# Transposing x by VectorE from a second load in 128-byte pieces: batches 2 and 3 of a fused attention and two-layer MLP kernel

## The chip, the cores and the metric

One core of a Trainium2 chip runs the kernel. The metric is the device time in microseconds (us) of one execution; of several runs the median is given. TensorE, VectorE, ScalarE, GpSimd (POOL) and SyncE (SP) each run their own queue of instructions in order, and wait for each other by semaphores. In the profile PE is TensorE's matmuls, PEld its weight loads, DVE is VectorE, ACT is ScalarE. DMAs are issued from the queues of SP and POOL.

## The reference

Attention between x and a small state in both directions, then two MLPs over all tokens, all in float32.

```python
# x: 4 x 8 x 512 x 64 (batch, head, token, channel), state: 4 x 8 x 32 x 64
scores  = softmax(x @ state.T / 8)        # per batch and head, 512 x 32
xread   = scores @ state                  # 512 x 64
scores2 = softmax(state @ x.T / 8)        # 32 x 512
sread   = scores2 @ x                     # 32 x 64
a = concat([xread, sread], axis=2)        # to 2176 tokens x 512
h = a @ moe_w_in;   a = (h - tanh(h)) @ moe_w_out          # 512 -> 2048 -> 512
h = a @ moe2_w_in;  out = (h * tanh(softplus(h))) @ moe2_w_out
```

## The kernel before

**The first half.** Work runs in steps. A step is one entry of the list `seq`: a batch b and one of 16 slices t of the hidden dimension of the first MLP. Batch 0 has steps 0 to 15, batch 1 steps 16 to 31, batch 2 steps 32 to 47; then come four steps for the state tokens and 16 for batch 3. In each step TensorE runs six matmuls into `h` (`up_x`, which reads the attention weights `ath`, `atl`) and twelve into four accumulators `acc0` to `acc3` (`down_x`, three steps behind). ScalarE computes tanh (`t`) and the rounded large part `gh`; VectorE computes h - tanh(h) (also `t`, or `wide` where the tile is half of a wide one) and the rest `gl`. At a batch's last step the four accumulators are copied to `y` (ScalarE acc0 and acc2, VectorE acc1 and acc3, `evac`). `h` alternates between two banks of PSUM; side work has two banks.

**Side work** is hung on the steps: `at(step, function)`. The attention of batches 2 and 3 is prepared while batch b - 1 runs, by the steps in `when[b]`, counted from that batch's first step (`start`). Of that preparation:

- `load_x(b)` loads x into four tiles `x`, one for each pair of heads k, by POOL.
- `at_xt(b, k)` transposes a tile: `xt_t` runs four 128x128 matmuls against an identity into a side bank `xtp`, `xt_c` copies the bank to `xt` (ScalarE, for batches 2 and 3).
- `sc_m(b)` computes the scores by sixteen 64x32 matmuls, alternating between two side banks (e = 0 and 1; `sct`), `sc_c` copies them to `scs`.
- `at_exp`, `at_norm`, `at_exp_t`, `at_read_t` and `at_sread` make both softmaxes and `sread` (`e2p`, `srd`); `sw` multiplies the state into the first weights (`swp`, split into `swh` and `swl` for the two banks). Only `at_sread` needs the x tile as it was loaded.

Weights of the second MLP are converted meanwhile: SP loads them to three stage buffers `st` (`load_next`), ScalarE reads a buffer twice (`w`, `r`), VectorE joins the two, and POOL stores the split parts (`wh`, `wl`) to DRAM (`wi`, `wo`). A load into a stage buffer waits until ScalarE has read what stood there. SBUF is kept in slots (`get`, `put`): a tile that takes a slot waits for those who last used it. DMAs of SP use eight semaphores in turn, so one waits until the eighth before it has landed.

**The second half** is the second MLP in 16 groups (`group`, `downs`), with weights loaded back from DRAM (`ws`, `wo`).

The order on each engine is that of a scheduler which follows the order of the code by priority; inside `sc_m` the matmuls after the first have a raised priority.

Of the kernel before, what the change touches and what calls it, by code (L numbers as in the profile page):

```python
# [10 lines left out]
F32 = mybir.dt.float32  # L11
# [65 lines left out]
def attention_moe_kernel(  # L77
# [10 lines left out]
    nc = tc.nc  # L88
# [5 lines left out]
    KD = DM // 128  # L94
# [3 lines left out]
    def order(after, before, cls=mybir.DependencyClass.NoSync):  # L98
        tc.add_manual_dep(
            after, before.name,  # L100
            mybir.DependencyInfo(cls, mybir.DependencyReason.DATA),
            reason="order of work",
        )

    TE, AC, V = (Pinned(e, order) for e in (nc.tensor, nc.scalar, nc.vector))
# [10 lines left out]
    free, halves = deque(range(NSLOT)), deque()  # L116
    wide = [slots.tile([128, 1024], F32, tag=f"v{i}", name="wide") for i in range(WIDE)]

    def get(name, dtype=F32, newest=False):
        if halves and dtype == F32:  # L120
            return halves.popleft()
        i = free.pop() if newest else free.popleft()
        return Unit(slots.tile([128, 512], dtype, tag=f"k{i}", name=name), i)

    def put(*units):
        for u in units:
            if u.slot is None:
                halves.append(u)
            else:
                free.append(u.slot)  # L130
# [4 lines left out]
    def side_bank(name):  # L135
        ps_n[0] += 1
        return psum.tile([128, 512], F32, tag=banks[ps_n[0] % len(banks)], name=name)

    ident = misc.tile([128, 128], F32, name="ident")
    SB = get("sbt")  # L140
    XS = get("xst")
    xst = XS.t.rearrange("p (k n) -> p k n", k=KD)

    SX = get("sx")

    def head(b, k, i, half=None):
        c = (b * KD + k) * NS
        p = i if half is None else half
        return (SB if p == i else SX).t[p * 64:(p + 1) * 64, c:c + NS]
# [259 lines left out]
    XT, SC, ET = {}, {}, {}  # L409

    def load_x(b, ks=range(KD)):
        for k in ks:
            u = get("x", newest=b > 1)
            (nc.gpsimd if b > 1 else nc.sync).dma_start(
                out=u.t.rearrange("p (h c) -> p h c", h=2),
                in_=x[b, 2 * k:2 * k + 2].rearrange("h (p r) d -> p h (r d)", r=4),
            )
            X[b, k] = u
# [5 lines left out]
    P = {}  # L424

    def v3(u):
        return u.rearrange("p (g n) -> p g n", n=NS)

    def xt_t(b, k):
        P["x", b, k] = ps = side_bank("xtp")  # L430
        for r in range(4):
            TE.transpose(
                out=ps[:, r * 128:(r + 1) * 128],
                in_=X[b, k].t[:, r * 128:(r + 1) * 128],
                identity=ident,
            )

    def xt_c(b, k):
        XT[b, k] = get("xt")
        evac(XT[b, k].t, P.pop(("x", b, k)), 0 if b else k)  # L440

    def at_xt(b, k):
        xt_t(b, k)
        xt_c(b, k)

    def sc_m(b):


        P["c", b] = [side_bank("sct") for _ in range(2)]
        before = None  # L450
        for i in range(2):
            for k in range(KD):
                for e in range(2):
                    with tc.high_priority() if before else nullcontext():
                        mm = TE.matmul(
                            out=P["c", b][e][k * NS:(k + 1) * NS, i * 256:(i + 1) * 256],
                            lhsT=head(b, k, i, e),
                            rhs=XT[b, k].t[e * 64:(e + 1) * 64, i * 256:(i + 1) * 256],
                            start=True,
                            stop=True,  # L460
                        ).ins
                    if before:
                        order(mm, before)
                    before = mm
        put(*(XT.pop((b, k)) for k in range(KD)))

    def sc_c(b, i):
        SC[b, i] = get("scs")
        for e in range(2):
            evac(  # L470
                SC[b, i].t.rearrange("p (q e n) -> p q e n", q=2, e=2)[:, :, e, :],
                P["c", b][e][:, i * 256:(i + 1) * 256].rearrange("p (q n) -> p q n", q=2),
                e if b else 1 - i,
            )

    def at_scores(b):
        sc_m(b)
        for j in range(2):
            sc_c(b, j)
# [34 lines left out]
    def at_exp(b, j):  # L514
        sc_t(b, j)
        sc_max(b, j)
        sc_sub(b, j)
        sc_exp(b, j)
# [19 lines left out]
    def at_norm(b, j):  # L538
        nm_sum(b, j)
        nm_rec(b, j)  # L540
        nm_mul(b, j)

    def at_exp_t(b, j):
        e = SC.pop((b, j))
        mt = small.tile([128, 2], F32, tag="mt", name="mt")
        V.tensor_reduce(out=mt[:, 0:1], in_=e.t, axis=AX.X, op=ALU.max)
        V.tensor_scalar(
            out=mt[:, 0:1], in0=mt[:, 0:1], scalar1=-scale, scalar2=None, op0=ALU.mult
        )
        AC.activation(  # L550
            out=e.t, in_=e.t, func=ACTF.Exp, scale=scale, bias=mt[:, 0:1], accum_out=mt[:, 1:2]
        )
        V.tensor_scalar(
            out=mt[:, 1:2], in0=mt[:, 1:2], scalar1=1e-9, scalar2=None, op0=ALU.add
        )
        V.reciprocal(out=mt[:, 1:2], in_=mt[:, 1:2])
        V.tensor_scalar(
            out=e.t, in0=e.t, scalar1=mt[:, 1:2], scalar2=None, op0=ALU.mult
        )
        ET[b, j] = e  # L560

    def at_read_t(b, j):
        ps = side_bank("e2p")
        e = ET.pop((b, j))
        for r in range(4):
            TE.transpose(
                out=ps[:, r * 128:(r + 1) * 128],
                in_=e.t[:, r * 128:(r + 1) * 128],
                identity=ident,
            )  # L570
        u = get("e2")
        AC.activation(out=u.t, in_=ps, func=ACTF.Copy)
        put(e)
        ET[b, j] = u
# [19 lines left out]
    def at_sturn(b):  # L594
        ps = side_bank("srt")
        u = P.pop(("r", b))
        TE.transpose(out=ps[:, :128], in_=u.t[:, :128], identity=ident)
        put(u)
        V.tensor_copy(
            out=xst[:, :, b * NS:(b + 1) * NS],  # L600
            in_=ps[:, :128].rearrange("p (k n) -> p k n", k=KD),
        )

    def at_steps(b):
        st = [lambda k=k: at_xt(b, k) for k in range(KD - 1)]
        return st + [
            lambda: at_xt(b, KD - 1),
            lambda: at_scores(b),
            lambda: (at_exp(b, 0), at_exp_t(b, 0)),
            lambda: at_norm(b, 0),  # L610
            lambda: (at_exp(b, 1), at_exp_t(b, 1), at_read_t(b, 0)),
            lambda: at_norm(b, 1),
            lambda: at_read_t(b, 1),
            lambda: at_sread(b),
            lambda: at_sturn(b),
        ]

    def at_a_hi(b, j):
        a = A.pop((b, j))
        if b >= TURN:  # L620
            u = get("at")
            V.transpose(out=u.t, in_=a.t)
            src = u.t
        else:
            u, src = None, side_bank("atp")
            for r in range(4):
                TE.transpose(
                    out=src[:, r * 128:(r + 1) * 128],
                    in_=a.t[:, r * 128:(r + 1) * 128],
                    identity=ident,  # L630
                )
        put(a)
        h = get("ath", F32R)
        last[0] = AC.activation(out=h.t, in_=src, func=ACTF.Copy).ins
        AT.setdefault(b, []).append((h, src, u))
# [85 lines left out]
    def evac(dst, src, i):  # L721
        if i % 2:
            return V.tensor_copy(out=dst, in_=src)
        return AC.activation(out=dst, in_=src, func=ACTF.Copy)
# [370 lines left out]
    def at(step, fn, back=None):  # L1095

        def held():
            kept = [e.floor for e in engines]
            for e, m in zip(engines, marks[-back]):
                e.floor = m  # L1100
            fn()
            for e, m in zip(engines, kept):
                e.floor = m

        side.setdefault(step, []).append(held if back else fn)

    seq = []
    start = {}
# [16 lines left out]
    for j in range(2):  # L1125
        at(12 + j, lambda j=j: at_exp(1, j))
        at(13 + j, lambda j=j: at_norm(1, j))
        for b in range(2):
            k = start[1] + 4 + 2 * b + 4 * j
            at(k, lambda b=b, j=j: at_exp_t(b, j), 1)  # L1130
            at(k + 3 - b, lambda b=b, j=j: at_read_t(b, j), 1)
            if j:
                at(k + 4 - b, lambda b=b: at_sread(b), 1)
                at(k + 5, lambda b=b: at_sturn(b), 1)
    when = {2: (3, 4, 5, 7, 8, 9, 10, 11, 12, 13, 15, 16), 3: (3, 3, 4, 5, 7, 8, 9, 11, 12, 12, 13, 15)}
    for b in (2, 3):
        at(start[b - 1] - (b - 2), lambda b=b: load_x(b))
        for i, f in zip(when[b], at_steps(b), strict=True):
            at(start[b - 1] + i, f)
    for b in (1, 2, 3):  # L1140
# [57 lines left out]
    st = {}  # L1198
# [145 lines left out]
```

## Time and profile before

| | |
|---|---|
| median of 3 runs (lowest, highest) | 709.61 us (708.37, 709.80) |
| the profiled execution's own time | 709.34 us |
| its span in the trace | 707.6 us |
| TensorE (PE) busy | 697.7 us, 99% of the span |
| VectorE, ScalarE, GpSimd busy | 472.7, 351.2, 70.7 us |
| mean DMA rate | 168 GB/s |

The time is the span and 1.7 us around it. Busy times of PE overlap: matmuls are pipelined, and one of 512 columns that takes 390 ns in the trace starts 227 ns after the one before it.

### The profile page before, as it was taken

To read this page: it belongs to the slowest core of one execution; us is meant where nothing else is said; L and a number is where in the kernel's file an instruction comes from. 1 tells how busy PE (TensorE), PEld (TensorE's weight loads), DVE (VectorE), ACT (ScalarE), POOL (GpSimd) and SP (SyncE) were. 2 spreads that over 40 slices of the span, in tenths; PEclk is the share of its full clock that TensorE was granted. 3 is DMA by queue.
4 is the path that set the end of the run, shared out by engine and by line. 5 is a ranking of instruction groups with operands and counts; after the bars stand their busy time and mean duration, and the time that the engine had idled before them with its cause. 6 is when DMAs were issued, how large, how long until landed. Compare 5 with 4: busy or idle time off the path is not lost.

```text
span 707.6 us, 10475 instructions
## 1 busy us (share of the span) xinstructions
PE 697.7 (99%) x3930; PEld 558.1 (79%) x3930; DVE 472.7 (67%) x809; ACT 351.2 (50%) x631; POOL 70.7 (10%) x110
## 2 busy tenths in 40 slices
PE   8899999999999999999999999999999999999998
PEld 6467777788777898778878888888888888888886
DVE  5899955778469757998466875557653456544654
ACT  6999544566575656866555432224333223212320
POOL 0000010006112423401213000000000000000000
PEclk9999999999999999999999999999999999999999
DMA  8985110017454568574949645443966345322003
GB/s 283 357 281 195 60 60 2 31 45 230 158 173 141 208 221 283 200 279 140 367 177 329 209 150 165 150 134 125 317 209 197 112 136 176 120 78 74 1 0 134
DMA packets 52643, 118.66 MB, mean 168 GB/s; under 512 B 7280, under 2 KB 11632, under 8 KB 52592
## 3 DMA queue, kind: packets, MB, share of 16 engines
q1 hardware_dynamic: 44272, 90.72, 38.0%
q0 software_dynamic: 8320, 27.27, 10.7%
q8 instruction: 31, 0.51, 0.3%
q14 instruction: 20, 0.16, 0.1%
HBM read 88.34 MB, written 29.62 MB: 167 GB/s over the span
## 4 chain that ended last, share of the span: by engine, by line
PE 84%; ACT 7%; DVE 5%; issue 1%; DMA 1%; SPq 1%; ACTq 0%; DVEq 0%
PE acc L64 47%; PE h L64 31%; ACT r L64 2%; ACT w L64 2%; PE hs L64 2%; PE swp L64 2%; DVE wide L64 1%; DMA x<-in_x_dram 1%; PE xtp L64 1%; DVE wl L64 1%; ACT gh L64 1%; DVE w L64 1%; ACT wide L64 1%; ACT t L64 1%; PE srd L64 1%
## 5 line engine op out<-in xcount | busy, mean ns | idle before, releaser
L64 PE MATMUL acc<-wo,gh 128*128 128x512 f32 (+1 forms) x548 | 168.0, 388 | 0.0
L64 PE MATMUL h<-yh,ws 128*128 128x512 f32 x448 | 156.7, 391 | 0.1
L64 PEld LDWEIGHTS acc<-wo,gh 128*128 128x128 f32 x548 | 102.1, 188 | 21.0 <-ACT gh L64 0.4
L64 DVE TENSOR_TENSOR wide<-acc,wide 128x512 f32<-128x512 f32 (+1 forms) x92 | 63.0, 684 | 74.5 <-PE acc L64 73.2
L64 PE MATMUL acc<-wo,gl 128*128 128x512 f32 (+1 forms) x274 | 106.3, 388 | 0.0
L64 PE MATMUL acc<-gh,wh 128*128 128x512 f32 x244 | 98.7, 404 | 0.0
L64 PEld LDWEIGHTS h<-yh,ws 128*128 128x128 f32 x448 | 84.1, 188 | 17.7 <-DVE mt L64 0.5
L64 PE MATMUL acc<-gh,wl 128*128 128x512 f32 x244 | 95.6, 392 | 0.0
L64 PE MATMUL acc<-gl,wh 128*128 128x512 f32 x244 | 95.1, 390 | 0.0
L64 PE MATMUL h<-yl,ws 128*128 128x512 f32 x224 | 87.2, 389 | 0.0
L64 DVE TENSOR_TENSOR wide<-h,wide 128x512 f32<-128x512 f32 x94 | 64.7, 688 | 25.1 <-PE h L64 13.2
L64 DVE TENSOR_TENSOR gl<-wide,gh 128x512 fp32r<-128x512 f32 x72 | 49.7, 691 | 47.4 <-ACT gh L64 47.2
L64 ACT ACTIVATE wide<-wide 128x512 f32<-128x512 f32 x47 | 29.7, 632 | 85.4 <-DVE wide L64 85.4
L64 ACT ACTIVATE wide<-h 128x512 f32<-128x512 f32 x41 | 24.4, 596 | 78.6 <-PE h L64 76.3
L64 PEld LDWEIGHTS acc<-wo,gl 128*128 128x128 f32 x274 | 51.4, 188 | 11.0 <-DVE gl L64 0.4
L64 PEld LDWEIGHTS acc<-gh,wh 128*128 128x128 f32 x244 | 45.8, 188 | 18.1 <-issue 4.6
L64 PEld LDWEIGHTS acc<-gh,wl 128*128 128x128 f32 x244 | 45.8, 188 | 11.3 <-issue 1.2
L64 PE MATMUL h<-ath,swh 128*128 128x512 f32 x128 | 51.6, 403 | 2.0 <-DVE t L64 1.0
L64 PEld LDWEIGHTS acc<-gl,wh 128*128 128x128 f32 x244 | 45.9, 188 | 8.6
L64 PE MATMUL h<-ath,swl 128*128 128x512 f32 x128 | 50.5, 395 | 0.1
L64 PE MATMUL h<-atl,swh 128*128 128x512 f32 x128 | 49.9, 390 | 0.0
L64 PEld LDWEIGHTS h<-yl,ws 128*128 128x128 f32 x224 | 42.1, 188 | 8.5
(175 smaller groups left out, 1019.6 us busy)
## 6 DMA issues: line engine op xcount, KB each, us to landing
ws<-wi SPq DMA_DIRECT2D x128, 256.0 KB, 3.8
wo<-wo SPq DMA_DIRECT2D x64, 256.0 KB, 3.8
st<-in_moe_w_in_dram SPq DMA_DIRECT2D x27, 512.0 KB, 5.7
st<-in_moe_w_out_dram SPq DMA_DIRECT2D x22, 512.0 KB, 4.9
wi<-wh POOLq DMA_DIRECT2D x32, 256.0 KB, 3.4
wi<-wl POOLq DMA_DIRECT2D x32, 256.0 KB, 4.6
wide<-in_moe_w_out_dram SPq DMA_DIRECT2D x10, 512.0 KB, 5.2
wo<-wh POOLq DMA_DIRECT2D x16, 256.0 KB, 5.8
```

Source lines behind the costliest of these rows:

```text
L64: i = fn(*args, **kw)
```

## The change

For batches 2 and 3 TensorE no longer transposes x. `load_xq` loads x a second time, in eight DMAs for each tile, all from SP: each fills 32 partitions with 256 pieces of 128 bytes, so that rows and columns of x stand in 32x32 blocks in places from which one VectorE transpose of 32x32 blocks (`xt_q`) makes `xt`, up to the order of the tokens. The copy of the scores (`sc_c`) puts the tokens back into order. The plain load of x, which `at_sread` still needs, comes eight steps later. In `sc_m` the two banks change places (e = 1 first) for these batches. In batch 3 the last three transposes stand one step later, and the first two no longer share one. The tiles `xq` and `at` don't take halves of wide tiles.

```diff
-    def get(name, dtype=F32, newest=False):
-        if halves and dtype == F32:
+    def get(name, dtype=F32, newest=False, whole=False):
+        if halves and dtype == F32 and not whole:
             return halves.popleft()
...
+    def load_xq(b, k):
+        u = get("xq", whole=True)
+        v = u.t.rearrange("p (i g d) -> p i g d", i=2, g=8)
+        for i in range(2):
+            src = x[b, 2 * k + i].rearrange("(l g e) (c d) -> (e c) l g d", g=8, e=2, c=2)
+            for c in range(4):
+                nc.sync.dma_start(out=v[c * 32:(c + 1) * 32, i], in_=src[c])
+        P["q", b, k] = u
+
+    def xt_q(b, k):
+        u = P.pop(("q", b, k))
+        XT[b, k] = get("xt")
+        V.transpose(out=XT[b, k].t, in_=u.t)
+        put(u)
...
-    def at_xt(b, k):
-        xt_t(b, k)
-        xt_c(b, k)
...
-                for e in range(2):
+                for e in (1, 0) if b > 1 else (0, 1):
...
                 e if b else 1 - i,
+            ) if b < 2 else evac(
+                SC[b, i].t.rearrange("p (q e l h) -> p q e l h", q=2, e=2, h=4)[:, :, e],
+                P["c", b][e][:, i * 256:(i + 1) * 256].rearrange("p (h q l) -> p q l h", h=4, q=2),
+                e,
             )
...
-        st = [lambda k=k: at_xt(b, k) for k in range(KD - 1)]
-        return st + [
-            lambda: at_xt(b, KD - 1),
+        return [lambda k=k: xt_q(b, k) for k in range(KD)] + [
             lambda: at_scores(b),
...
-            u = get("at")
+            u = get("at", whole=True)
...
-    when = {2: (3, 4, 5, 7, 8, 9, 10, 11, 12, 13, 15, 16), 3: (3, 3, 4, 5, 7, 8, 9, 11, 12, 12, 13, 15)}
+    when = {2: (3, 4, 5, 7, 8, 9, 10, 11, 12, 13, 15, 16), 3: (3, 4, 5, 6, 7, 8, 9, 11, 12, 12, 13, 15)}
     for b in (2, 3):
-        at(start[b - 1] - (b - 2), lambda b=b: load_x(b))
+        for k in range(KD):
+            at(start[b - 1] + when[b][k] - 3, lambda b=b, k=k: load_xq(b, k))
+        at(start[b - 1] + 8 - (b - 2), lambda b=b: load_x(b))
```

**TensorE at the scores of batch 2** (step 24; `h_1471` and `h_1479` are the same h before and after, `sct_1499`, `sct_1516` the bank that is written first). Before:

```order
L64 MATMUL h_1471<-ath_1140,swl_1409 128x512
L64 MATMUL e2p_1485<-ident_75,scs_373 128x128 x4
L64 MATMUL sct_1499<-wide_72,sbt_76 32x256
L64 MATMUL acc0_1293<-gh_1357,wh_629 128x512
L64 MATMUL acc0_1293<-gl_1358,wh_629 128x512
L64 MATMUL sct_1500<-wide_72,sx_78 32x256
L64 MATMUL sct_1499<-wide_72,sbt_76 32x256
```

and with the change:

```order
L64 MATMUL h_1479<-ath_1140,swl_1422 128x512
L64 MATMUL e2p_1493<-ident_75,scs_373 128x128 x4
L64 MATMUL acc0_1307<-gh_1375,wh_629 128x512
L64 MATMUL acc0_1307<-gl_1376,wh_629 128x512
L64 MATMUL acc0_1307<-gh_1375,wl_630 128x512
L64 MATMUL acc1_1308<-gh_1375,wh_629 128x512
L64 MATMUL sct_1516<-wide_72,sx_78 32x256
L64 MATMUL sct_1515<-wide_72,sbt_76 32x256
```

Before, two acc matmuls stood between the first sct matmul and the other fifteen; now four acc matmuls stand ahead of all sixteen.

**VectorE at the end of batch 1** (steps 34 and 35; `y` is the copied accumulator, `xq_2102` batch 3's tile k = 1). Before:

```order
L64 TENSOR_TENSOR swl_2136<-swp_2122,swh_2135 128x512
L64 TENSOR_TENSOR gl_2118<-wide_72,gh_2117 128x512
L64 TENSOR_TENSOR swl_2132<-swp_2121,swh_2131 128x512
L64 COPY y_2146<-acc1_1294 128x512
L64 COPY y_2156<-acc3_1296 128x512
L64 SCALAR_TENSOR_TENSOR w_2204<-w_2204,r_2205 128x512
```

and with the change:

```order
L64 TENSOR_TENSOR swl_2163<-swp_2149,swh_2162 128x512
L64 TENSOR_TENSOR gl_2145<-wide_72,gh_2144 128x512
L64 TENSOR_TENSOR swl_2159<-swp_2148,swh_2158 128x512
L64 COPY wide_72<-acc1_1308 128x512
L64 STREAM_TRANSPOSE xt_2270<-xq_2102 128x512
L64 COPY y_2191<-acc3_1310 128x512
L64 SCALAR_TENSOR_TENSOR w_2236<-w_2236,r_2237 128x512
```

A transpose, and with it the wait for xq_2102's DMAs, now stands ahead of the copy of acc3.

**SP from batch 1's first steps to batch 2's fourth** (`xq_1178`, `1216`, `1268`, `1343` are k = 0 to 3 of batch 2, `xq_2053`, `2102`, `2166`, `2209` those of batch 3, `st` weight loads). Before, the loads st_950, 993, 1041, 1125 and 1537 followed each other here. With the change:

```order
L193 DMA st_950<-in_moe2_w_in_dram 128x1024
L437 DMA xq_1216<-in_x_dram 32x8x32 x2
L437 DMA xq_1178<-in_x_dram 32x8x32 x8
L437 DMA xq_1216<-in_x_dram 32x8x32 x6
L437 DMA xq_1268<-in_x_dram 32x8x32 x8
L437 DMA xq_1343<-in_x_dram 32x8x32 x8
L193 DMA st_993<-in_moe2_w_in_dram 128x1024
L193 DMA st_1041<-in_moe2_w_out_dram 128x1024
L437 DMA xq_2166<-in_x_dram 32x8x32 x8
L437 DMA xq_2209<-in_x_dram 32x8x32
L437 DMA xq_2053<-in_x_dram 32x8x32
L193 DMA st_1125<-in_moe2_w_out_dram 128x1024
```

The next rows are st_1553, xq_2053 x7, xq_2102 x8, xq_2209 x5, st_1779, one of xq_2209, st_2024, st_2033 and the last of xq_2209. So all of batch 2's pieces stand between two weight loads, and those of batch 3 stand among the loads and behind what these wait for.

## Rows read from the trace of the kernel before

**Rows 1.** The page, part 1: busy time, share and instructions of each engine.

```profile
PE 697.7 (99%) x3930; PEld 558.1 (79%) x3930; DVE 472.7 (67%) x809; ACT 351.2 (50%) x631; POOL 70.7 (10%) x110
```

**Rows 2.** Windows: PE, PEld, DVE, ACT, POOL busy (count), clock, DMA, GB/s.

```profile
103.00:137.00 34.00, 34.00 (x197) 26.13 (x196) 21.02 (x45) 18.54 (x37) 0.00 (x0) 1.00 0.06 17
171.00:209.00 38.00, 38.00 (x225) 28.97 (x224) 22.19 (x39) 21.90 (x41) 8.98 (x14) 1.00 0.50 173
```

**Rows 3.** Timeline of PE (start, duration): first h of steps 16, 17, 19, 20.

```profile
90.62 0.39 PE L64 MATMUL h<-ath,swh 128*128 128x512 f32 x1
94.70 0.39 PE L64 MATMUL h<-ath,swh 128*128 128x512 f32 x1
...
104.12 0.39 PE L64 MATMUL h<-ath,swh 128*128 128x512 f32 x1
108.70 0.39 PE L64 MATMUL h<-ath,swh 128*128 128x512 f32 x1
```

**Rows 4.** Timeline of PE: step 35 and the start of step 36.

```profile
185.21 0.39 PE L64 MATMUL h<-ath,swh 128*128 128x512 f32 x1
...
186.34 0.39 PE L64 MATMUL h<-ath,swl 128*128 128x512 f32 x1
...
187.37 0.47 PE L64 MATMUL acc<-gh,wh 128*128 128x512 f32 x1
...
190.21 0.39 PE L64 MATMUL h<-ath,swh 128*128 128x512 f32 x1
```

**Rows 5.** Timeline of PE: step 24 and the start of step 25.

```profile
128.15 0.39 PE L64 MATMUL h<-ath,swh 128*128 128x512 f32 x1
...
130.04 0.62 PE L64 MATMUL sct<-wide,sbt 64*32 64x256 f32 x2
...
134.71 0.39 PE L64 MATMUL h<-ath,swh 128*128 128x512 f32 x1
```

**Rows 6.** Timeline of PE: first h of steps 39 and 40.

```profile
204.66 0.39 PE L64 MATMUL h<-ath,swh 128*128 128x512 f32 x1
...
209.99 0.39 PE L64 MATMUL h<-ath,swh 128*128 128x512 f32 x1
```

**Rows 7.** Lines by form (busy us, mean ns), and one tile's (ns min/median/max).

```profile
L64 DVE STREAM_TRANSPOSE a<-wide 128x512 f32<-128x512 f32 x2 | 1.4, 707 | 0.8 <-PE h L64 0.8
L64 ACT ACTIVATE xt<-xtp x6: 592/594/606, 115.3 to 196.8; 128x512 f32<-128x512 f32 x6
```

**Rows 8.** Timeline of DVE: t of steps 19 and 20; copies to y.

```profile
106.38 0.69 DVE L64 TENSOR_TENSOR wide<-h,wide 128x512 f32<-128x512 f32 x1 [1.25 <-ACT wide L64]
...
110.95 0.69 DVE L64 TENSOR_TENSOR wide<-h,wide 128x512 f32<-128x512 f32 x1
...
184.94 1.28 DVE L64 COPY y<-acc 128x512 f32<-128x512 f32 x2
```

**Rows 9.** Tile x: SP's issues (ns), landing; DMA from 1.5 to 2.5 us.

```profile
L414 SPq DMA_DIRECT2D x<-in_x_dram x8: 462/562/1516, 1.2 to 8.0; - x8
DMA to landing us min/median/max: 3.0/4.7/7.8
q1 hardware_dynamic: 523, 0.13, 58.2%
```

**Rows 10.** The page, part 3: packets, MB, share of 16 engines.

```profile
q1 hardware_dynamic: 44272, 90.72, 38.0%
```

**Rows 11.** Timeline of PE: last h of step 15, first of step 22.

```profile
87.68 0.39 PE L64 MATMUL h<-ath,swl 128*128 128x512 f32 x1
...
117.81 0.39 PE L64 MATMUL h<-ath,swh 128*128 128x512 f32 x1
```

**Rows 12.** Timeline of SP's queue, 149 to 170 us: three loads merged.

```profile
150.02 19.43 SPq L193 DMA_DIRECT2D st<-in_moe_w_out_dram  x3
```

**Rows 13.** DMA issues, 160 to 186 us: KB each, median us to landing.

```profile
x<-in_x_dram POOLq DMA_DIRECT2D x3, 256.0 KB, 7.7
wide<-in_x_dram POOLq DMA_DIRECT2D x1, 256.0 KB, 6.9
```

## The prediction

> **What bounds the kernel now.** I read the page first, then the windows, then TensorE's timeline. TensorE is busy for 697.7 of 707.6 us [rows 1]. In the two stretches in which batches 2 and 3 are prepared, 103 to 137 and 171 to 209 us, it is busy for every microsecond at the full granted clock (1.00, the 2.4 GHz level), while VectorE is busy for 21.0 of 34 and 22.2 of 38 us [rows 2]. So in these stretches time goes only if TensorE's instructions go, and it is lost only if TensorE is made to wait. Idle VectorE or DMA time saved would be worth nothing.
>
> The period of a step shows what an instruction of TensorE costs, better than its own duration, since matmuls overlap. A plain step (12 matmuls into acc, 6 into h) runs from 90.62 to 94.70, 4.08 us; step 19, with one group of four x transposes, from 104.12 to 108.70, 4.58 us [rows 3]. Step 35 has two groups in a row: 185.21 to 190.21, 5.00 us [rows 4]. So a group costs about 0.48 us, and the second of a pair 0.44.
>
> **What is removed from TensorE.** Eight groups: three alone in batch 2 and one behind an e2p group (which I count as a second of a pair), a pair and two alone in batch 3. That is 5 x 0.48 + 0.44 + 0.92 = 3.76 us. I see no gain beyond that, and little below it: what follows a group in the queue simply moves up.
>
> **The scores.** In batch 2 they are split today: one sct matmul starts at 130.04, two acc matmuls slip in, then the other fifteen run. Step 24 takes 6.56 us, 128.15 to 134.71 [rows 5]. Batch 3 has the scores in one piece and no e2p group: step 39 takes 5.33 us, 204.66 to 209.99 [rows 6]. With 0.48 for the e2p group, an unsplit step 24 would take 5.81, so the split costs 0.75 us. In the changed order four acc matmuls come first and all sixteen sct follow together. That removes the split: bound 0 (the wait for the bank stays) to 0.75; I take 0.75, because four acc matmuls are 0.9 us of cover for the one copy that the first sct waits for.
>
> **What is added beside TensorE.** VectorE gets eight 128x512 transposes at 0.71 us each, 5.7 us; ScalarE loses eight copies of 0.59 us [rows 7]. VectorE has 12.98 and 15.81 us free in the two stretches, so their sum costs nothing; only their places count. What it costs to read the scores in a new element order no row shows: between nothing and, as a bound, one transpose more for each of the eight reads, 0.71 us; they are off TensorE and have several steps of cover, so I take nothing.
>
> One place has no cover. At the end of batch 1 VectorE copies acc1 and then acc3 to y, from 184.94 to 186.22 [rows 8]. Step 35's h ends 0.23 us after its last start at 186.34, at 186.57, and today two transpose groups follow, so that acc starts at 187.37 [rows 4]. Batch 2's first acc is acc3. With the groups gone acc3 is wanted at 186.57, and the order puts a transpose between the two copies: acc3 is then free at about 184.94 + 3 x 0.62 + 0.1 = 186.9. I charge 0.35 us of wait (bounds 0 and 0.7).
>
> **The loads.** Each tile of x comes a second time as eight DMAs of 32 KB, 256 pieces of 128 bytes, all on SP. SP is in order, and a piece waits for the landing of the eighth DMA before it. Call p the time per 32-KB DMA at which this stream runs. Issue bounds it below: SP's issues of x tiles, which also have 256 descriptors, take 0.46 at least, 0.56 in the median; I take 0.56. Data alone gives less: in the stretch in which the state's 256-byte pieces come, 523 packets keep 16 engines 58.2% busy for 1 us, 17.8 ns each, so 256 take 0.28 us [rows 9]. Eight in flight with a landing of 4.7 us (median for x tiles [rows 9]) give 0.59. The far end is a mean packet of the HW queue, 38.0% of 16 x 707.6 us over 44272 packets, 97 ns: 256 of them take 1.55 us [rows 10]. That packet has 2 KB, so I stand near the low end.
>
> In batch 2 all 32 DMAs stand together. The first tile is held until step 15's h ends, 87.68 + 0.23 = 87.9 [rows 11]. The tile with least room is xq_1268, the 24th DMA: 87.9 + 24 x 0.56 + 4.7 = 106.0, and VectorE wants it after t of step 19, at 107.1 [rows 8]. Being late costs nothing at first: t of step 20 ends at 111.6 [rows 8], and its bank is wanted by step 22's h at 117.8 [rows 11], 6.2 us of cover.
>
> In batch 3 fifteen DMAs of k = 0 and 1 are queued behind the load st_1553, which waits for ScalarE to have read a stage buffer. Its counterpart today is issued by 169.45, the end of the group of three [rows 12]. So xq_2102 lands at 169.5 + 15 x 0.56 + 4.7 = 182.6, and VectorE wants it at 184.94 + 0.62 = 185.6, just before the acc3 copy. 3 us of room, and behind them no cover. The last piece of k = 3 stands behind st_2033, which waits for a conversion by ScalarE in step 35; VectorE wants it behind gl of step 36, a step (4.1 us) later, against a landing of 4.7: late by half a microsecond, with a step of cover through the h banks. The plain load of x (POOL), now later, serves only srd, six steps or more on.
>
> Here the Trainium skill speaks against the change: "DMA: Bandwidth & Descriptors", Specifications, wants 512 bytes per piece for line rate, and its Rules for kernel authors say that under 64 KB one pays mostly overhead. The trace agrees as far as it goes: 256 bytes in 17.8 ns are 14 GB/s an engine, 2 KB in 97 ns are 21; no row shows 128-byte pieces. If I took that page's 0.95 us for a 64 KB transfer (its section Bandwidth, Measured) for each of these DMAs, an estimate, the sum would end where it began, near 709.
>
> **Sum**, on the profiled execution's 709.34 us (span 707.6 and 1.74 around it; the median of the runs is 0.27 higher): 709.34 - 3.76 - 0.75 + 0.35 = 705.2; half the offset of the median gives **705.3 us**, 0.6% faster.
>
> **Rivals.**
> *A little late (13%).* In 160 to 186 us x tiles took 6.9 and 7.7 us to land beside the stores [rows 13]. Eight in flight at 6.9 give p = 0.86, and xq_2102 lands at 169.5 + 12.9 + 6.9 = 189.3, 3.7 late, all of it on TensorE: 708.9. At 5.8, between: p = 0.73, 186.2, 0.6 late, 705.8. For it: this stretch has the stores. Against: today's slow landings are whole 256-KB tiles, and these four plain loads have left the stretch.
>
> *Slower (8%).* The small pieces themselves are the limit. With p = 1.55, xq_1268 lands at 129.8, 22.7 late less 6.2 of cover, and xq_2102 at 197.5, 11.9 late: 705.2 + 16.5 + 11.9 = 733.6. It decides from p near 0.95: then xq_1268 is 8.3 late, 2.1 beyond its cover, xq_2102 is 2.9 late, and 5.0 lost is more than the 4.2 won. Against: the 256-byte row is at 0.28.
>
> *The gain does not arrive (9%).* TensorE speeds up but meets ScalarE or VectorE waits that the slower pace hid, above all where ScalarE converts weights in order in front of tanh (st_1779 and st_2024 are used soon after they are issued). Half the gain lost gives 707.3, all 709.4. Against: no such wait stands in either stretch now, and an h bank has over a step of room.
>
> **Chances.** Forecast 70%, between 704.3 and 706.3 on its own. A measurement of this kernel tells about 0.2%, 1.4 us, from no change. Faster takes the forecast, and about half of "late" and of "does not arrive": 0.82. Same: the rest of these two, 0.10. Slower: 0.08. For 8 in 10 I give 704.0 to 708.2: below, the waits at nought and 0.4 of run-to-run spread; above, half of the two middle rivals.
>
> **What would show it.** Right: steps 19 to 23 and 35 to 37 at 4.1 us; no sct split, step 24 near 5.8; one wait for acc3's copy below 0.7 us. xq landing within 3 to 6 us, and VectorE's idle before its transposes on xq short. Wrong: an acc wait of microseconds near 185, VectorE idle behind a DMA of xq, SP issues of xq spaced by 0.9 us or more, or new TensorE waits after 210.

## The result and the profile after

The changed kernel takes 714.5 us in the median (713.4 to 717.7); before, on the same chip, 709.7 (708.4 to 710.8). The ratio is 1.007, 95% interval 1.0051 to 1.0089: slower by 0.7%, where 0.6% faster was forecast. The profiled execution took 714.7 us with a span of 712.9, 5.3 more than before. The page's first line, part 1 and part 3, against [rows 1] and [rows 10]:

```profile
span 712.9 us, 10511 instructions
PE 695.7 (98%) x3898; PEld 554.8 (78%) x3898; DVE 476.7 (67%) x817; ACT 346.1 (49%) x623; POOL 70.7 (10%) x110
q1 hardware_dynamic: 61680, 92.82, 40.6%
```

TensorE works 2.0 us less in a span 5.3 us longer, so it stands idle 7.3 us more. The timeline of PE says where. First the kernel before, h of steps 31 and 41 (its other steps are in [rows 3] to [rows 6]):

```profile
166.12 0.39 PE L64 MATMUL h<-ath,swh 128*128 128x512 f32 x1
...
214.07 0.39 PE L64 MATMUL h<-ath,swh 128*128 128x512 f32 x1
```

Then the changed kernel: h of steps 16, 24, 25, 31, 35, 36, 39, the first scores of batch 3, and h of steps 40 and 41.

```profile
90.30 0.39 PE L64 MATMUL h<-ath,swh 128*128 128x512 f32 x1
...
125.95 0.39 PE L64 MATMUL h<-ath,swh 128*128 128x512 f32 x1
...
131.75 0.39 PE L64 MATMUL h<-ath,swh 128*128 128x512 f32 x1
...
163.14 0.39 PE L64 MATMUL h<-ath,swh 128*128 128x512 f32 x1
...
182.23 0.39 PE L64 MATMUL h<-ath,swh 128*128 128x512 f32 x1
...
188.21 0.39 PE L64 MATMUL h<-ath,swh 128*128 128x512 f32 x1
...
201.71 0.39 PE L64 MATMUL h<-ath,swh 128*128 128x512 f32 x1
...
204.90 0.62 PE L64 MATMUL sct<-xt,sx 64*32 64x256 f32 x2 [1.67 <-DVE swl L64]
206.29 0.63 PE L64 MATMUL sct<-xt,sbt 64*32 64x256 f32 x1 [0.78 <-DVE swl L64]
...
211.67 0.39 PE L64 MATMUL h<-ath,swh 128*128 128x512 f32 x1
...
215.75 0.39 PE L64 MATMUL h<-ath,swh 128*128 128x512 f32 x1
```

Differences of such starts give the time by stretch in us (e5 and e9 are two of the experiments below, read in the same way):

| stretch | before | after | e5 | e9 |
|---|---|---|---|---|
| start to step 16 | 90.62 | 90.30 | 89.69 | 89.82 |
| step 16 to 31 (batch 2 prepared) | 75.50 | 72.84 | 72.84 | 72.83 |
| step 31 to 35 | 19.09 | 19.09 | 19.09 | 19.10 |
| step 35 to 41 (batch 3 prepared) | 28.86 | 33.52 | 28.86 | 26.98 |
| step 41 to the end | 493.5 | 497.2 | 492.1 | 493.0 |

Batch 2 gives 2.66 us, as reckoned. Batch 3's stretch should have given 1.9 and loses 4.7; behind it 3.6 more are lost. The chain of waits of PE (us in total, times, longest) from 160 to 260 and from 260 to 420 us has four lines, all of them new:

```profile
PE sct L64 <- DVE swl L64: 2.4, 2, 1.7
PE acc L64 <- DVE y L64: 1.6, 1, 1.6
PE h L64 <- DVE t L64: 3.2, 1, 3.2
PE h L64 <- DVE wide L64: 0.8, 1, 0.8
```

In each TensorE waits for VectorE. In the sct wait and the long h wait VectorE is late because ScalarE is; the short one of 0.8 us, at 316 us, isn't followed up here. ScalarE's and VectorE's timelines ahead of the sct wait and of the h wait (start, duration, idle time before and what ended it), with the store that POOL issued in between:

```profile
196.26 0.63 ACT L64 ACTIVATE wh<-w 128x512 fp32r<-128x512 f32 x1 [2.54 <-DMA wo<-wh]
...
197.18 0.71 POOL L262 DMA_DIRECT2D wi<-wh  x1 [4.66 <-ACT wh L64]
...
202.38 0.67 ACT L64 ACTIVATE w<-st 128x512 f32<-128x512 f32 x1 [3.62 <-DMA wi<-wh]
202.95 0.57 ACT L64 ACTIVATE t<-h 128x512 f32<-128x512 f32 x1
203.56 0.69 DVE L64 TENSOR_TENSOR t<-h,t 128x512 f32<-128x512 f32 x1 [3.66 <-ACT t L64]
204.17 0.68 DVE L64 TENSOR_TENSOR swl<-swp,swh 128x512 fp32r<-128x512 f32 x1
...
284.45 0.63 ACT L64 ACTIVATE yh<-wide 128x512 fp32r<-128x512 f32 x1 [5.63 <-DMA wo<-wl]
```

The conversion at 202.38 writes its w into a buffer from which a store of wh is still on its way; it waits 3.62 us for the landing. The tanh (t at 202.95) stands behind it in ScalarE's order, VectorE's t waits 3.66 us for the tanh, swl stands behind t, and the scores want the bank that swl reads. The 3.2 us at 283 us are the same: ScalarE waits 5.63 us for a store to leave the buffer that yh is to take. Of the view of ScalarE's waits between 150 and 300 us, two lines of before and then five of after, its own for landings and the tanh's for TensorE:

```profile
ACT t L64 <- PE h L64: 12.2, 8, 2.9
...
ACT w L64 <- DMA wi<-wl: 1.8, 1, 1.8
```

```profile
ACT yh L64 <- DMA wo<-wl: 5.6, 1, 5.6
...
ACT w L64 <- DMA wi<-wh: 3.6, 1, 3.6
ACT t L64 <- PE h L64: 3.3, 3, 2.5
ACT w L64 <- DMA st<-in_moe_w_in_dram: 3.3, 2, 3.1
...
ACT wh L64 <- DMA wo<-wh: 2.5, 1, 2.5
```

All lines of that view together: ScalarE waits 2.3 us for DMAs before and 18.1 after (13.6 of them for stores to leave a buffer, 4.5 for weight loads), and its tanh waits for TensorE's h 12.2 us before and 3.3 after. The slack that ScalarE had against TensorE has gone into these waits, most of them for buffers.

The acc wait has another root. VectorE, SP and ScalarE from 168 to 185 us:

```profile
168.39 15.82 SPq L437 DMA_DIRECT2D xq<-in_x_dram  x20
...
178.75 0.71 DVE L64 STREAM_TRANSPOSE xt<-xq 128x512 f32<-128x512 f32 x1 [3.00 <-DMA xq<-in_x_dram]
...
180.13 0.60 ACT L64 ACTIVATE wide<-h 128x512 f32<-128x512 f32 x1 [3.72 <-DVE gl L64]
...
183.96 0.70 DVE L64 STREAM_TRANSPOSE xt<-xq 128x512 f32<-128x512 f32 x1
184.59 0.65 DVE L64 COPY y<-acc 128x512 f32<-128x512 f32 x1
```

The first tile of batch 3 (k = 0) lands late; VectorE stands 3.00 us with gl queued behind the transpose, ScalarE waits 3.72 us for gl, and all the copies of acc behind it move. The second transpose, at 183.96, finds its data there.

### The profile page after: what moved, and what is told of

It is laid out like the page before. It is cut to its first block, busy times and chain, and to the rows that moved or that the text cites. A ratio compares the mean times of both kernels' runs of the same rounds, so it can differ in the third digit from the quotient of the medians.

```text
span 712.9 us, 10511 instructions
## 1 busy us (share of the span) xinstructions
PE 695.7 (98%) x3898; PEld 554.8 (78%) x3898; DVE 476.7 (67%) x817; ACT 346.1 (49%) x623; POOL 70.7 (10%) x110
## 4 chain that ended last, share of the span: by engine, by line
PE 68%; issue 11%; ACT 7%; DVE 6%; POOL 5%; DMA 2%; SPq 0%; POOLq 0%; DVEq 0%
PE acc L64 38%; PE h L64 26%; POOL wi L262 3%; ACT r L64 2%; ACT w L64 2%; PE hs L64 2%; POOL wo L262 1%; DMA wo<-wl 1%; PE swp L64 1%; ACT gh L64 1%; DVE a L64 1%; ACT t L64 1%; DMA x<-in_x_dram 1%; DVE wl L64 1%; DVE wide L64 1%
## 5 line engine op out<-in xcount | busy, mean ns | idle before, releaser
L64 DVE TENSOR_TENSOR wide<-h,wide 128x512 f32<-128x512 f32 x97 | 66.6, 687 | 27.3 <-ACT wide L64 13.3
L64 DVE TENSOR_TENSOR gl<-wide,gh 128x512 fp32r<-128x512 f32 x75 | 51.6, 689 | 45.6 <-ACT gh L64 45.2
L64 ACT ACTIVATE wide<-h 128x512 f32<-128x512 f32 x44 | 26.1, 595 | 86.3 <-PE h L64 81.7
L64 ACT ACTIVATE gh<-wide 128x512 fp32r<-128x512 f32 x75 | 47.3, 632 | 12.0 <-DVE wide L64 10.2
```

What stands on the lines that cost most here:

```text
L64: i = fn(*args, **kw)
```

## The experiments

One thing shows only when the program is written out. The conversion of the second MLP's weights is cut into 94 pieces, and a piece is run in a step only while `done[0] < goal and bg and len(free) >= RESERVE` (RESERVE is 10): it is held back when buffers are few. The plain load of batch 3's x, moved from step 31 to step 39, leaves its buffers free longer. So the pieces run earlier: 20 instead of 15 are done at step 36, 26 instead of 21 at step 39, 48 instead of 40 at step 48, 59 instead of 48 at step 51. Counted from the program, without a run, it would be 17, 23, 43 and 52 with only batch 3's plain load moved back: the moved load accounts for about three fifths of the earlier pieces, the rest of the change in batch 3 for the others. My theory after reading the traces was that these earlier pieces are the loss; the rivals were the 128-byte pieces and the swapped order of the scores.

**e1, e2: whose schedule of pieces.** Both have a table in place of the test, e1 (on the changed kernel) with the numbers of before, e2 (on the kernel before) with those of after:

```diff
-                    if done[0] < goal and bg and len(free) >= RESERVE:
+                    if done[0] < ran_by[i] and bg:
```

> The changed kernel, with the weight-conversion pieces run at the same steps as in the kernel before (a table of how many have run by each step, in place of the test on free buffers); loads and transposes of x as changed. If the time was lost because freer buffers let the pieces run earlier (by 5 at step 39, 8 at step 48, 11 at step 51): 706 to 708 us, without the sct waits near 204 us (2.4), the fall of the granted clock after them and the h wait near 283 us (3.2). If the 128-byte pieces are the cause, or the swapped order of the scores: 713 to 715, the sct waits still there.

Measured: 710.2 us, ratio 1.0011 (0.9999 to 1.0024). So 4.4 us come back, but not the gain, and the time lies between the two ranges. The waits near 185 and 204 us shrink to 1.1 each and the one at 283 is gone, but a new one of 3.8 stands at 227:

```profile
PE e2p L64 <- DVE swl L64: 3.8, 1, 3.8
PE sct L64 <- DVE swl L64: 1.1, 1, 1.1
PE acc L64 <- ACT w L64: 1.1, 1, 1.1
```

> The kernel before, with the conversion pieces run at the steps at which the changed kernel runs them; nothing else of the change. If the earlier pieces are the cause: slower than before by 2 to 6 us (712 to 716), with TensorE waits near 200 to 210 and 280 to 290 us. If the cause is in the 128-byte pieces or the order of the scores: 709 to 710, no new wait.

Measured: 722.1 us, ratio 1.0177 (1.0164 to 1.0190), a loss twice as large as the most that I expected. The waits are of the same kind, but end at 190 and 233 us and not where I looked for them (PE, 160 to 260 us):

```profile
PE xtp L64 <- DVE swl L64: 3.3, 1, 3.3
PE e2p L64 <- DVE swl L64: 2.5, 1, 2.5
```

From 150 to 300 us ScalarE waits 18.8 us for stores in e2, 2.0 in the kernel before, and nothing but the steps of the pieces differs. The longest of these waits:

```profile
ACT yh L64 <- DMA wo<-wl: 6.4, 1, 6.4
```

That the earlier pieces cost time is shown in both directions. They aren't the whole: with before's schedule the change still gives nothing.

**e3, e12: the size of the pieces.** Second loads in runs of 1 KB, with after's schedule (e3) and with before's (e12); both leave out the right order of x:

```diff
-            src = x[b, 2 * k + i].rearrange("(l g e) (c d) -> (e c) l g d", g=8, e=2, c=2)
+            src = x[b, 2 * k + i].rearrange("(c l q) (g d) -> c l (q g) d", c=4, l=32, g=2)
```

> The changed kernel, with the same number of second loads of x and the same bytes, but each read and written in runs of 1 KB instead of 128 bytes; the scores of batches 2 and 3 are then computed on a wrongly ordered x. If the small pieces are the cause: 705 to 708, all three groups of waits gone. If the earlier conversion pieces are: 712 to 715, with the waits near 204 and 283 us still there, and at most the 1.6 us on acc3's copy gone.

Measured: 719.2 us, ratio 1.0133 (1.0116 to 1.0149), above both ranges.

> As e1, with the second load of x in runs of 1 KB instead of 128 bytes (same number of loads and bytes; the scores of batches 2 and 3 are computed on a wrongly ordered x). If the 128-byte pieces cost anything here: 705 to 708. If they don't: 709 to 711.5, with the same kinds of waits.

Measured: 711.7 us, ratio 1.0032 (1.0021 to 1.0043), against e1's 1.0011. SP's issues of batch 2's 32 loads, e1 and then e12 (start, duration of the whole):

```profile
88.71 21.64 SPq L437 DMA_DIRECT2D xq<-in_x_dram  x32
```

```profile
88.84 15.98 SPq L437 DMA_DIRECT2D xq<-in_x_dram  x32
```

Larger runs bring the time of a load from 0.68 to 0.50 us, and the kernel is no faster for it. The small pieces are not the cause. (Why e3 is slower still than the changed kernel stays unexplained.)

**e4: the order of the scores.** `for e in range(2)` in both batches.

> The changed kernel, with the two banks of the scores written in the order of before (e = 0 first) in both batches. If the swapped order costs the sct waits near 204 us: 710 to 711. If not: 713 to 716, the waits on swl moved to the other bank but not gone, and in batch 2 the scores split again (0.75 us).

Measured: 716.8 us, ratio 1.0112 (1.0091 to 1.0134), just above the second range. The sct wait is 3.0 us, and step 24 takes 6.52 us again (h at 127.28 and 133.80). The swap is worth having.

**e5, e6: one batch alone.** e5 keeps the change in batch 2 and gives batch 3 back its plain loads at step 31 and its TensorE transposes; e6 is the reverse, with before's schedule of pieces:

```diff
-        return [lambda k=k: xt_q(b, k) for k in range(KD)] + [
+        return [lambda k=k: (xt_q if b == 2 else at_xt)(b, k) for k in range(KD)] + [
```

> The change in batch 2 alone; batch 3 has its x transposed by TensorE and loaded when it was before. The free buffers then let the conversion pieces run at the steps of the kernel before by themselves. If all that is lost is lost by what the change does in batch 3's stretch (160 to 290 us): 709.6 less 2.6 (four groups, 1.9, and the split of the scores, 0.75), 706.5 to 707.5. If a faster TensorE meets waits of ScalarE and VectorE wherever it comes earlier: 709 to 711.

Measured: 705.7 us, ratio 0.9943 (0.9929 to 0.9958), the fastest of the versions that leave nothing out: faster than before by 0.6%, than the change as made by 1.2%, and a little below the range that I gave. No wait of TensorE is listed from 90 us on. It is 3.6 us earlier at step 41 (0.9 of it from the stretch before step 16, where the change has no part) and wins another 1.4 behind, 1.0 of it a wait of acc on VectorE that the kernel before has at 271 us.

> The change in batch 3 alone, batch 2 as before, with the conversion pieces at the steps of the kernel before. If the two halves add up: e1's 710.2 plus the 2.6 that batch 2 gives, 712 to 713.5, with a wait of 3 to 4 us near 227 us. If batch 3's part only loses when TensorE comes 2.6 us earlier: 707.5 to 709.

Measured: 714.3 us, ratio 1.0068 (1.0049 to 1.0086), with 5.0 us of wait at e2p: above both ranges. The two halves add: by the ratios, -4.0 and +4.8 us make e1's +0.8. So the loss lies in batch 3's part, whether TensorE comes earlier or not.

**e7, e8, e11: three remedies on e1.** e7 issues the plain loads as early as before:

```diff
-        at(start[b - 1] + 8 - (b - 2), lambda b=b: load_x(b))
+        at(start[b - 1] - (b - 2), lambda b=b: load_x(b))
```

> As e1 (both batches changed, conversion pieces at the steps of the kernel before), but the plain load of x is issued on the POOL queue as early as in the kernel before, at steps 16 and 31 in place of 24 and 39. If the plain loads that now stand among the stores on POOL make the stores late, and these ScalarE's conversions (a store's landing ended 3.1 us of ScalarE's waiting at 217 us in e1, and TensorE then waited 3.8 us at 227 us): 705 to 707. If they don't matter: 709.5 to 711, the wait near 227 us still there.

Measured: 709.2 us, ratio 0.9998 (0.9987 to 1.0008). The wait at 227 us is gone; one of 3.3 us that ends at 187 us stands instead, acc on y, and behind it TensorE runs at half clock. Step 35 takes 10.09 us for e9's 4.08 (e9 follows below), and these 6.0 us are all that the trace of e7 loses against that of e9 from step 16 on. The y wait goes back to a buffer: ScalarE stands until 177 us for a store, VectorE's gl behind it, and the copies to y behind gl; the transpose's own wait for xq, 0.55 us, is the smaller part. ScalarE's wait:

```profile
ACT r L64 <- DMA wi<-wh: 5.8, 1, 5.8
```

The late plain loads are worth about 0.9 us, which is not clear of the noise: the intervals of e7 and e1 overlap.

> As e1, but a buffer whose store has been issued goes back to the free ones after 10 pieces instead of 6, so that it is written again later. If ScalarE waits because buffers are written again while their stores are on the way: the waits on landings of wo<-wh and wi<-wl (3.1 and 2.5 us of ScalarE's in e1) go or shrink below 1 us, and the time is 705.5 to 708. If what is late is the loads of weights or of x: 709.5 to 711.

`HOLD = 10` measured: 711.0 us, ratio 1.0019 (1.0008 to 1.0030). ScalarE waits 2.6 and 2.0 us for stores of wi. Holding the buffers of stores longer is no help; that it leaves fewer others may be why, but isn't shown.

> As e1, but the conversion pieces are held back further while batch 3's second load runs: 12 of them done at step 39 instead of 21 (26 in the changed kernel), caught up by step 49. If the second load and the conversions collide (buffers, loads of weights, ScalarE): the waits near 185, 204 and 227 us go, 704 to 706, unless the catching up costs as much. If the cause lies in the transposes or the loads themselves: 709 to 712.

The table of e1 with 12 from step 32 to step 39, rising to 40 at step 49. Measured: 711.5 us, ratio 1.0026 (1.0015 to 1.0038); the waits near 185 and 204 us are gone (0.3 left), but 2.1 us at e2p (227 us) and 2.6 on wide (273 us) have come in the steps in which the pieces are caught up and behind them. So less work at once helps there and costs later.

**e9, e10: no second load in batch 3.** VectorE transposes the plainly loaded tiles, which come at step 31 again; e10 also takes the buffers of the second load, unused:

```diff
-        V.transpose(out=XT[b, k].t, in_=u.t)
+        V.transpose(out=XT[b, k].t, in_=(u if b == 2 else X[b, k]).t)
...
+        if b == 3:
+            P["q", b, k] = None
+            return
```

> As e1 (both batches changed, conversion pieces at the steps of the kernel before), but batch 3 has no second load: x is loaded plainly as early as in the kernel before, and VectorE transposes those tiles, so batch 3's scores are computed on a wrongly ordered x. TensorE's, ScalarE's and VectorE's work is that of the changed kernel. If the second load of batch 3 (its traffic, its buffers, its place among the weight loads on SP) is what costs: e5's 705.7 less the 1.9 of four groups, 703 to 704.5, no TensorE wait above 0.5 us in 160 to 300 us. If the four transposes on VectorE, among its conversions, or the order of the scores cost it: 708 to 711, with waits near 185 or 227 us.

Measured: 703.4 us, ratio 0.9918 (0.9904 to 0.9931), inside what the second load as cause predicts. TensorE's h of steps 16, 35 and 41:

```profile
89.82 0.39 PE L64 MATMUL h<-ath,swh 128*128 128x512 f32 x1
...
181.75 0.39 PE L64 MATMUL h<-ath,swh 128*128 128x512 f32 x1
...
208.73 0.39 PE L64 MATMUL h<-ath,swh 128*128 128x512 f32 x1
```

> As e9, but the four buffers of the second load are taken and given back as in the changed kernel, with nothing loaded into them, so that four fewer are left for the conversions in steps 32 to 38. If buffers are what batch 3's second load costs: 708 to 710, near e7's 709.2, with ScalarE waiting for landings of stores. If its traffic or its place in SP's queue is: 703 to 705, as e9.

Measured: 706.8 us (704.0 to 709.7), ratio 0.9958 (0.9942 to 0.9975): between the two. Taking four buffers, with nothing loaded into them, costs about 2.8 us; the executions spread by 5.7 us, so this size is rough. How it costs them is not shown. The trace, of an execution of 704.8 us, has one wait of TensorE from 90 us on, and it isn't behind a conversion: VectorE's first transpose of batch 3 now stands ahead of a copy that srt needs (it starts at 170.61, in e9 at 173.64) and waits for its plain tile (PE, then DVE):

```profile
PE srt L64 <- DVE wide L64: 1.4, 1, 1.4
```

```profile
DVE xt L64 <- DMA wide<-in_x_dram: 2.3, 1, 2.3
```

ScalarE waits 3.4 us for stores (0.6 in e9) and 8.0 for weight loads (3.2), but TensorE waits for none of these. So e10 also changes the order on VectorE, and its slower executions have no trace.

**e13, e14: the rest of the second load.** On e7: one DMA of 256 KB a tile in batch 3 instead of eight (e13); each tile asked for two steps ahead instead of three (e14). The edit of e14:

```diff
-            at(start[b - 1] + when[b][k] - 3, lambda b=b, k=k: load_xq(b, k))
+            at(start[b - 1] + when[b][k] - (5 - b), lambda b=b, k=k: load_xq(b, k))
```

> As e7 (plain x early, conversion pieces at the steps of the kernel before), but batch 3's second load takes one DMA of 256 KB a tile instead of eight of 32 KB: 4 issues on SP instead of 32, the same bytes and the same four buffers (batch 3's scores are computed on a wrongly ordered x). If what the second load costs beyond its buffers (e10 706.8 to e7 709.2) is SP's issuing, in front of the weight loads: 706 to 707.5. If it is the traffic, or the waiting of the transposes for it: 708.5 to 710.

Measured: 709.4 us, ratio 0.9999 (0.9984 to 1.0013). An eighth of the issues brings no gain; VectorE's transpose now waits 5.1 us for its tile, which may hide one:

```profile
DVE xt L64 <- DMA xq<-in_x_dram: 5.1, 1, 5.1
```

> As e7, but each tile of batch 3's second load is asked for two steps ahead of its transpose instead of three, so that its buffer is held a step (4.1 us) less, and SP is held by it later. If the buffers held are the main cost: 706.5 to 708.5. If it is that the transposes wait for late landings, which stand in front of the copies of acc: 710 to 713, with a wait on y near 185 us longer than e7's 3.3.

Measured: 707.2 us, ratio 0.9963 (0.9951 to 0.9975), 2.5 us better than e7 though VectorE waits 4.7 us in all for the tiles; the wait on y is 0.7.

## Why the prediction was wrong

In ratios to before, times 709.7, the runs make one chain from before to after (in another order the parts can come out otherwise): change in batch 2, -4.0 us (e5); batch 3's exchange of TensorE for VectorE, -1.8 (e9); the four slots of its second load, +2.8 (e10); the rest of that load, +2.8 (e7, which also has batch 2's plain load early); the plain load later, +0.9 (e1, not certain); the pieces that run earlier for it, +4.2 (after).

*TensorE's terms: right.* Eight groups at 3.76 and the split at 0.75. From step 16 to 31 it is 2.66 us for 2.63 reckoned, from step 35 to 41 in e9 1.88 for 1.88; step 24 takes 5.80 for 5.81. That idle VectorE time would take the transposes for nothing holds too: e9 has all eight.

*The step that failed* is the sentence on the plain load, that it "now later, serves only srd, six steps or more on": I looked at who reads the load and priced its move at nothing. Its buffers, and the four of the second load, stand in no term of the sum; for the second load I charged the 0.35 us of acc3 alone. Both act on the pool from which every conversion takes its buffers. The later load does most to open the gate for the pieces: in steps 35 and 36 together the kernel before runs one, the changed one six. That the earlier pieces cost the +4.2 is shown by e1 and, on the kernel before, by e2. That the second load of batch 3 costs 5.6 us in all is shown by e9 and e7, and e7's trace shows the way: a conversion that takes a buffer with a store on the way, 5.8 us, and TensorE's 3.3 us and half clock behind it. That half of it is the price of four buffers rests on e10 alone, whose trace shows another way.

*The loads: the mechanism right, the size off, the tile wrong.* The time per DMA is 0.67 in batch 2 (21.52 us for 32) and 0.79 in batch 3 (15.82 for 20) instead of 0.56. The tile looked at, k = 1, is there when VectorE comes; the one that is late is k = 0, whose last seven pieces go out behind st_1553 and have landed only at 178.75. I didn't look at that one; gl stands behind it, and ScalarE behind gl. The wait for acc3 is 1.6 us for 0.35 (bounds 0 and 0.7). One sum was a slip: with the 5.0 us that the rival "Slower" reckons for 0.95 us per DMA the time is 710, not "near 709".

*The rivals.* "Slower", the small pieces as the limit: refuted by e12. There the Trainium skill's page "DMA: Bandwidth & Descriptors" (Specifications, 512 bytes per piece for line rate) agrees with the trace in direction, 0.68 us against 0.50 for 32 KB, but the time of the kernel doesn't hang on it. "A little late" is true of the acc3 wait alone, and by another tile. "The gain does not arrive" named the place, ScalarE's conversions in order in front of tanh. But it took the faster TensorE as the cause, and stopped at the loss of the whole gain. e5 shows TensorE earlier by 3.6 us with no such wait, and e2 shows 12.5 us lost with nothing of TensorE's changed. The waits behind the earlier pieces come without any gain, and so aren't bounded by it.

What stays open: why the pieces cost 12.5 us on the kernel before but 4.2 on the changed one, and how the 5.6 us of the second load divide between buffers, changed order, traffic and the transposes' waits; e13 speaks against SP's issuing, no more. The number of free buffers alone doesn't decide: counted from the programs, at step 36 the kernel before has 8 free, e9 9, e10 and e7 7, but e1 11, and e1 is not faster than e7.

## What to carry to other kernels

A load that is moved or added takes and frees buffers, and where other work is let in by a count of free buffers, it moves that work; so write out what the gate lets through at each step, before and after, and price it like an instruction that was moved (4.2 and 12.5 us here). An in-order engine that was found waiting for the bound engine has slack only until something ahead of it in its queue takes a buffer whose store is still on the way: list the buffers' last users for the stretch. And try such a change batch by batch, since here one half wins 4.0 us and the other loses 4.8.

## What was not expected of the hardware

A short wait of TensorE can cost more than itself. After the sct waits of the changed kernel (2.45 us idle between 203 and 206.3 us) the granted clock falls from 1.00 to 0.50, the level of 1.2 GHz, and is back before 211 us; windows of PE (busy us, clock, DMA share, GB/s):

```profile
203.00:205.00 2.00, 0.33 (x3) 1.00 0.31 84
205.00:207.00 2.00, 1.23 (x18) 0.79 0.89 295
207.00:209.00 2.00, 2.00 (x24) 0.50 0.88 266
209.00:211.00 2.00, 2.00 (x9) 0.86 0.73 279
```

By these rows 0.42 + 1.00 + 0.28 = 1.7 us are lost beside the 2.45, and step 39 takes 9.96 us for the 5.33 of before. In e7, behind the 3.3 us of wait, the clock is 0.50 from 187 to 193 us, and step 35 takes 10.09 us; in e1, behind the 3.8 us of wait, it is 0.50 from 229 to 231 us. But behind the 3.2 us of wait at 283 us of the changed kernel it stays at 1.00:

```profile
283.00:286.00 3.00, 0.12 (x1) 1.00 0.26 104
286.00:288.00 2.00, 1.66 (x14) 1.00 0.02 4
```

So the length of one wait alone doesn't tell, by these rows, whether the clock will fall.
